# Masks built first, small loads moved, more multiplications by zero and a new order table in a window-attention and gated-convolution kernel

## The chip, the cores and the metric

The kernel runs on one NeuronCore of a Trainium2 chip. The time is that of the device, in microseconds (us), from one launch. The engines are TensorE (PE in the profile; its weight loads are a row of their own, PEld), VectorE (DVE), ScalarE (ACT), GpSimd (POOL) and SyncE (SP), which here only issues DMAs. Each engine works through its own queue in order; semaphores tie the queues together.

## The reference

Attention with four sink positions and a window of 128 for 4 batches, 8 heads, 768 positions and head size 64, and behind it a causal convolution of five taps whose sigmoid gates a projection:

```python
scores = scale * np.matmul(q, k.transpose(0, 1, 3, 2))
keep = is_sink | in_window            # pos < 4, or 0 <= row - col < 128
a = softmax(np.where(keep, scores, -1e9))
x = np.matmul(a, v)                   # heads side by side: [4, 768, 512]
gate = sigmoid(sum(conv_w[k] * x shifted by 4 - k))
val = x @ w_val
out = (gate * val) @ w_out
```

All of it in float32. n_sink and window are inputs too; the kernel computes a flag that says whether they are 4 and 128, and a general path, not taken here, stands behind it.

## The kernel before

The work is cut into 24 steps: batch (4) x blocks of 256 positions (3) x halves of the heads (2). A step has two score groups, 0 and 1. For a group, PE makes the scores of the window in 16 matmuls per pair of heads (line 298) into **one** buffer of PSUM (`ss`); DVE overwrites one triangle by a predicated copy with the mask `low` (line 303) and adds the mask and takes the row maximum in four custom operations (line 308); ACT takes four exponentials (line 316). For the step, DVE makes the reciprocal of the sums (lines 321, 322), POOL normalises (lines 330, 334), PE transposes the weights (line 346) and the sink columns (line 351), DVE applies the masks `cur` and `prev` to the transposes (lines 362, 364), ACT copies the rest (lines 355, 371), and PE multiplies by the values (lines 384, 392) into **one** buffer `xv`. ACT copies that (lines 403, 407), writes four columns of the step before at its head (line 411), POOL takes the low part of the split (line 417) and the last tap (line 421), and DVE makes four taps of the convolution from `xv` (line 429, eight operations), before ACT's tanh (line 434).

Two steps (both halves of the heads) make a pair `m`. For a pair, PE makes the projection in four parts of twelve matmuls (line 448, v0 to v3), DVE multiplies by the gate (line 459), ACT and POOL split the product in two (lines 463, 467), and PE makes the output in four parts of six (line 478, o0 to o3); ACT copies it out (line 482) and SP stores it.

The weights come as raw words of eight bytes, four chunks for each of `w_val` and `w_out`. A decode in six stages (a to f) turns each chunk into a high and a low part: ACT (line 126), three DVE operations (lines 129, 130, 132), ACT and POOL (lines 139, 140), ACT (line 135), three matmuls (lines 149 to 151), ACT (line 154). The conv weights go through a smaller decode.

The order of everything is written out by numbers. Every piece of work (a score group, a reciprocal, a load, a decode stage) is an event with a time in units of steps: `WHEN` holds the usual offset of each kind, `EARLY` the exceptions for the first and last steps, `DECODE` those of the weight chunks. The events are sorted by that number and issued in that order, so the table sets each engine's queue. Masks are an event at -9.0. In front of the events PE gets six multiplications by zero (`busy`, line 181: 128x512, bf16, results unused), and two more stand behind each score group of the first three steps. The scalars n_sink and window and the conv weights are loaded through ACT's queue before everything else.

Of the kernel before, what the change touches and what calls it, by code (L numbers as in the profile page):

```python
# [11 lines left out]
I32 = mybir.dt.int32  # L12
# [21 lines left out]
WHEN = dict(kq=-2.002, vv=1.145, s0=-0.314, e0=0.342, s1=-0.127, e1=0.504, rec=0.668, norm=0.824, tx=1.127,  # L34
            ty=1.242, sk=1.124, ev=1.474, yv=1.657, ts=1.464, val=1.842, xc=1.965, xh=2.125, hd=2.131, xl=2.311,
            c4=2.096, c0=2.268, c1=2.39, th=2.762, v0=0.37, v1=0.378, v2=0.467, g0=0.558, v3=0.567, h0=0.774,
            l0=0.947, g1=0.823, h1=1.166, l1=1.291, o0=1.375, o1=1.538, o2=1.683, t0=2.094, o3=1.887, t1=2.281,
            cw=-5.891)

EARLY = {("kq", 0): -16.694, ("vv", 0): -0.872, ("s0", 0): -8.688, ("e0", 0): -3.333, ("s1", 0): -2.548,  # L40
# [28 lines left out]
DECODE = {("wv", "l"): (-36.913, -5.959, -16.477, -1.322), ("wv", "a"): (-36.852, -1.816, -3.87, 0.468),  # L69
# [90 lines left out]
def banded(ctx, tc, wts, cw, zero, ident, flag, qt, kt, vt, vsk, w_val, conv_w, w_out, out):  # L160
# [357 lines left out]
    with tc.manual_schedule():  # L518
        for _, f, args in sorted(events, key=lambda e: e[0]):
            f(*args)  # L520
            if f is scores and args[0] < BUSY:
                busy(2)
# [200 lines left out]
```

## Time and profile before

| what | value |
|---|---|
| median of 3 runs | 293.2 us (292.97 to 293.42) |
| profiled execution, its own time | 292.72 us |
| its span, first to last instruction | 290.9 us |
| mean granted TensorE clock | 0.981 |
| PE busy | 269.0 us, 92% |
| DVE busy | 209.2 us, 72% |
| ACT busy | 179.0 us, 62% |
| POOL busy | 157.2 us, 54% |

Reading the rows: in the timeline the first number is the start in us from the beginning of the span, the second the duration; then engine, line, operation, what is written from what, shapes, and in brackets the idle time of the engine before it and what ended that. In a list of waits the three numbers are the total in us, the count and the longest. A window's row has its bounds and length, then each engine's busy time with its count of instructions, the granted clock, the DMA share and GB/s.

### The profile page before, as it was taken

How to read it: one execution, taken by the hardware profiler on the slowest of the kernel's cores; microseconds unless marked ns; L12 is line 12 of the kernel's file. 1: busy time of each engine (PE TensorE's matmuls, PEld its weight loads, DVE VectorE, ACT ScalarE, POOL GpSimd, SP SyncE). 2: the span in 40 equal slices, each digit the busy share in tenths (PEclk: the TensorE clock that was granted, in tenths of full speed). 3: DMA queues.
4: the chain of work that ended last, by engine and by line, in shares of the span. 5: the costliest groups of instructions: out<-in, count | busy, mean ns of one | idle time of the engine just before them, and what ended most of it. 6: DMA issues, size and time to landing. Idle time of an engine off the chain costs nothing. (4 is left out here: it accounts for less than half of the span.)

```text
span 290.9 us, 8754 instructions
## 1 busy us (share of the span) xinstructions
PE 269.0 (92%) x3304; PEld 222.9 (77%) x3306; DVE 209.2 (72%) x797; ACT 179.0 (62%) x613; POOL 157.2 (54%) x193
## 2 busy tenths in 40 slices
PE   3648989999999999999999999999999999999981
PEld 0324656979988879889889789899898798897860
DVE  0586899988598589687886976985885777858500
ACT  2277798686478468467655854774694676573410
POOL 2234667575555663863764564556638638645330
PEclk9966999999999999999999999999999999999999
DMA  3957926033335326418317334353362080140102
GB/s 118 362 193 244 299 94 197 7 98 91 132 96 169 114 90 200 137 38 274 98 52 227 94 128 152 97 163 116 94 183 97 2 275 2 45 139 1 74 11 72
DMA packets 27393, 36.90 MB, mean 127 GB/s; under 512 B 2256, under 2 KB 23760, under 8 KB 27344
## 3 DMA queue, kind: packets, MB, share of 16 engines
q1 hardware_dynamic: 26912, 36.25, 38.8%
q8 instruction: 28, 0.46, 0.7%
q14 instruction: 21, 0.17, 0.2%
q10 hardware_dynamic: 432, 0.02, 0.1%
HBM read 29.97 MB, written 6.29 MB: 125 GB/s over the span
## 5 line engine op out<-in xcount | busy, mean ns | idle before, releaser
L330 POOL TENSOR_TENSOR wx<-w,sm 128x512 f32<-128x512 f32 x48 | 49.2, 1047 | 73.4 <-DVE sm L322 69.8
L429 DVE SCALAR_TENSOR_TENSOR sg<-xv,cw,sg 128x256 f32<-128x256 f32 x192 | 77.4, 474 | 2.7 <-ACT xv L411 2.7
L316 ACT ACTIVATE w<-sx,ngm 128x132 f32<-128x132 f32 x192 | 74.9, 395 | 1.6 <-DVE ngm L308 1.6
L298 PE MATMUL ss<-k,q 64*64 64x200 f32 x768 | 45.8, 355 | 10.9 <-DMA q<-in_qt_dram 4.7
L403 ACT ACTIVATE xt<-xv 128x512 f32<-128x512 f32 x24 | 14.3, 597 | 64.9 <-PE xv L392 64.8
L303 DVE COPY_PREDICATED ss<-low,ss 128x256 f32<-128x256 uint8 x48 | 20.5, 426 | 43.6 <-PE ss L298 42.9
L448 PE MATMUL acc<-xh,wvh 128*128 128x256 f32 x192 | 49.1, 289 | 0.0
L448 PE MATMUL acc<-xh,wvl 128*128 128x256 f32 x192 | 47.9, 279 | 0.0
L308 DVE CUSTOM_DVE_ANT_0 sx<-ss,mask 128x132 f32<-128x132 f32 x192 | 45.2, 292 | 1.7
L298 PEld LDWEIGHTS ss<-k,q 64*64 64x64 f32 x768 | 27.0, 137 | 21.2 <-issue 10.7
L478 PE MATMUL acc<-woh,gh 128*128 128x512 f32 x96 | 40.2, 419 | 0.1
L478 PE MATMUL acc<-woh,gl 128*128 128x512 f32 x96 | 38.2, 398 | 0.6 <-POOLq L656 0.6
L478 PE MATMUL acc<-wol,gh 128*128 128x512 f32 x96 | 38.0, 396 | 0.0
L316 ACT ACTIVATION_READ_ACCUMULATOR w<-sx,ngm 128x1 f32 x192 | 36.7, 191 | 0.0
L448 PEld LDWEIGHTS acc<-xh,wvl 128*128 128x128 f32 x192 | 36.4, 190 | 0.1
L448 PEld LDWEIGHTS acc<-xh,wvh 128*128 128x128 f32 x192 | 36.0, 188 | 0.1
L467 POOL TENSOR_TENSOR gl<-sg,gh 128x512 fp32r<-128x512 f32 x24 | 30.9, 1286 | 8.1 <-ACT gh L463 6.9
L421 POOL TENSOR_TENSOR sg<-xt,cw 128x512 f32<-128x512 f32 x24 | 25.2, 1051 | 16.0 <-ACT xt L403 16.0
L392 PE MATMUL xv<-wt,v 64*64 64x192 f32 (+2 forms) x1024 | 33.3, 273 | 0.0
L392 PEld LDWEIGHTS xv<-wt,v 64*64 64x64 f32 x1024 | 31.6, 133 | 0.9
L448 PE MATMUL acc<-xl,wvh 128*128 128x256 f32 x192 | 31.1, 282 | 0.3 <-POOL xl L417 0.3
L417 POOL TENSOR_TENSOR xl<-xt,xh 128x512 fp32r<-128x512 f32 x24 | 31.0, 1293 | 0.2 <-ACT xh L407 0.2
(103 smaller groups left out, 422.3 us busy)
## 6 DMA issues: line engine op xcount, KB each, us to landing
k<-in_kt_dram SPq DMA_DIRECT2D x23, 408.0 KB, 4.0
v<-in_vt_dram SPq DMA_DIRECT2D x16, 384.0 KB, 4.5
out_dram<-osb SPq DMA_DIRECT2D x24, 256.0 KB, 2.7
q<-in_qt_dram SPq DMA_DIRECT2D x23, 256.0 KB, 4.3
raw<-in_w_val_dram SPq DMA_DIRECT2D x4, 512.0 KB, 6.4
raw<-in_w_out_dram SPq DMA_DIRECT2D x4, 512.0 KB, 5.8
v<-in_vt_dram SPq DMA_DIRECT2D x8, 256.0 KB, 4.2
vs<-in_vsk_dram SPq DMA_DIRECT2D x8, 128.0 KB, 4.1
```

The source lines that it names most:

```text
L298: nc.tensor.matmul(ss[e * D:(e + 1) * D, j, c * n:(c + 1) * n], q[js, g, (2 * c + e) * D:(2 * c + e + 1) * D], k[js, g, (2 * c + e) * HB:( ...
L303: nc.vector.copy_predicated(sv[:, :, :, :D], low[:, None, None, :].to_broadcast([P, 2, 2, D]), sv[:, :, :, 2 * HB:])
L308: nc.vector.tensor_tensor_reduce(out=sx[:, j, c], in0=sv[:, j, c, :PK], in1=mask[:, c if p == 0 else 2], op0=ALU.add, op1=ALU.min, scale=- ...
L316: nc.scalar.activation(out=w[:, g, j, c], in_=sx[:, j, c], func=AF.Exp, scale=-1.0, bias=ngm[:, g, j, c:c + 1], accum_out=sm[:, g, j, c:c ...
L330: nc.gpsimd.tensor_tensor(out=t[:, n].rearrange("p c h x -> p h c x"), in0=w[:, :, :, at], in1=sm.to_broadcast([P, 4, 2, D]), op=ALU.mult)
L392: nc.tensor.matmul(acc[o * D:(o + 1) * D, g, x0 + h * D:x0 + (h + a1 - a0 + 1) * D], v[js, g, n], t[js, g, n, a0:a1 + 1].rearrange("p a r ...
L417: nc.gpsimd.tensor_tensor(out=xl[:, g], in0=xts[s], in1=xh[:, g].bitcast(F32), op=ALU.subtract)
L421: nc.gpsimd.tensor_tensor(out=sg[s // 2][:, g], in0=xts[s], op=ALU.mult, in1=cw[:, g, KT - 1:].to_broadcast([P, 2, PQ]))
L429: nc.vector.scalar_tensor_tensor(out=g, in0=x, scalar=a, in1=g, op0=ALU.mult, op1=ALU.add)
L448: nc.tensor.matmul(acc[:, h], a[:, kc, cs], x[:, kc], start=(n == 0), stop=(n == 11))
L467: nc.gpsimd.tensor_tensor(out=gl, in0=g, in1=gh.bitcast(F32), op=ALU.subtract)
L478: nc.tensor.matmul(acc, a[:, kc, ts], x[:, kc], start=(kc + n == 0), stop=(kc + n == 5))
```

## The change

- The masks (lines 216 to 241) become the very first event (-133.1 instead of -9.0).
- The loads of n_sink and window become an event at 6.6, and the load of the conv weights an event at -31.4, behind the keys and queries of step 0; all go through SP's queue instead of ACT's. The flag comes at 21.4 instead of 24.6.
- Multiplications by zero: 16 in front instead of 6; then 6 behind the first score group, 5 behind the total of the first value chunk, 8 behind the first group of step 1 and 2 behind the total of the second value chunk, instead of 2 behind each of six score groups. That is 37 instead of 18.
- All numbers of `WHEN`, `EARLY` and `DECODE` are new. In the steady steps the order of the kinds changes in a few places; over the first four steps it changes in many.

```diff
-WHEN = dict(kq=-2.002, vv=1.145, s0=-0.314, e0=0.342, s1=-0.127, e1=0.504, rec=0.668, norm=0.824, tx=1.127,
...
+WHEN = dict(kq=-1.097, vv=-0.039, s0=-0.08, e0=0.57, s1=-0.026, e1=0.45, rec=0.712, norm=0.815, tx=1.002, ty=1.129,
...
-BUSY = 3
...
+FIRST = 16
+
+FILL = {("scores", (0, 0)): 6, ("decode_weights", ("wv", 0, 4)): 5, ("scores", (1, 0)): 8,
+        ("decode_weights", ("wv", 1, 4)): 2}
 LAG = 3
...
-def _scalars(nc, pool, n_sink, window):
-
-    raw = pool.tile([P, 2, 2], I32, name="nw_raw")
+def _scalars(nc, raw, n_sink, window):
+
     for k, ap in enumerate((n_sink, window)):
         src = ap.bitcast(I32).rearrange("(o n) -> o n", o=1)
-        nc.scalar.dma_start(out=raw[:, k, :], in_=src.to_broadcast([P, 2]))
-    return raw
+        nc.sync.dma_start(out=raw[:, k, :], in_=src.to_broadcast([P, 2]))
...
-    nc.scalar.dma_start(out=craw, in_=conv_w.bitcast(I32).rearrange("p (m t) -> p m t", t=2))
+
+    def load_conv():
+        nc.sync.dma_start(out=craw, in_=conv_w.bitcast(I32).rearrange("p (m t) -> p m t", t=2))
...
-    events += [(-9.0, masks, ()), (24.6, flag, ()), (WHEN["cw"], conv_weights, ())]
+    events += [(-133.108, masks, ()), (6.559, scalars, ()), (21.43, flag, ()), (-31.442, load_conv, ()), (WHEN["cw"], conv_weights, ())]
...
-    busy(6)
+    busy(FIRST)
     for t in skb:
         nc.gpsimd.memset(t, 0.0)
     with tc.manual_schedule():
         for _, f, args in sorted(events, key=lambda e: e[0]):
             f(*args)
-            if f is scores and args[0] < BUSY:
-                busy(2)
+            if (f.__name__, args) in FILL:
+                busy(FILL[f.__name__, args])
```

Line numbers of the changed kernel are one higher from the scores on and one lower in the masks and the decode.

What the new numbers do to the queues, first on POOL at the start of the program, before (`mk` holds the iotas of the masks, `wv_f` is the decode product of the first value chunk):

```order
L245 TENSOR_SCALAR plus<-ident 128x128
L246 TENSOR_SCALAR minus<-ident 128x128
L140 TENSOR_TENSOR wv_f<-wv_e,wv_p 128x512
L219 IOTA mk 64x64 x2
L222 IOTA mk 128x64
L140 TENSOR_TENSOR cw_f<-cw_e,cw_p 128x20
```

and in the change:

```order
L218 IOTA mk 64x64
masks.py:199 AFFINE_SELECT ident<-ident 128x128
L218 IOTA mk 64x64
L244 TENSOR_SCALAR plus<-ident 128x128
L245 TENSOR_SCALAR minus<-ident 128x128
L221 IOTA mk 128x64
L139 TENSOR_TENSOR wv_f<-wv_e,wv_p 128x512
```

The three iotas have moved ahead of the decode product. On DVE at the same place, before (the first decode's three operations, then the first of the masks):

```order
L641 MEMSET warm 128x1
L129 TENSOR_SCALAR wv_t<-wv_p 128x512
L130 SCALAR_TENSOR_TENSOR wv_t<-wv_p,wv_t 128x512
L132 TENSOR_SCALAR wv_e<-wv_t 128x512
L220 CAST mk<-mk 128x64
L221 TENSOR_SCALAR low<-mk 128x64
```

and in the change (the last of the masks, the first decode, the first score group):

```order
L237 TENSOR_SCALAR mask<-mask 128x396
L239 TENSOR_SCALAR cur<-mk 128x64
L240 TENSOR_SCALAR prev<-mk 128x64
L128 TENSOR_SCALAR wv_t<-wv_p 128x512
L129 SCALAR_TENSOR_TENSOR wv_t<-wv_p,wv_t 128x512
L131 TENSOR_SCALAR wv_e<-wv_t 128x512
L304 COPY_PREDICATED ss<-low,ss 128x2x2x64
```

All of the masks have moved ahead of the first decode, and the first score group follows that decode directly. Behind it DVE had the conv weights and a second chunk's decode ahead of the second score group; in the change the second group follows the first directly, then come the conv weights and two chunks' decodes.

The third place is DVE in a steady step with output products, before (the convolution, then the transposes' products, then the reciprocal):

```order
L308 ISA ngm 128x1
L429 SCALAR_TENSOR_TENSOR sg<-xv,cw,sg 128x256 x8
L362 TENSOR_TENSOR wt<-tr,cur 128x2x4x64
L364 TENSOR_TENSOR wt<-tr,prev 128x2x4x64
L321 TENSOR_SCALAR sm<-sm 128x8
L322 RECIPROCAL sm<-sm 128x8
```

and in the change:

```order
L309 ISA ngm 128x1
L363 TENSOR_TENSOR wt<-tr,cur 128x2x4x64
L365 TENSOR_TENSOR wt<-tr,prev 128x2x4x64
L430 SCALAR_TENSOR_TENSOR sg<-xv,cw,sg 128x256 x8
L322 TENSOR_SCALAR sm<-sm 128x8
L323 RECIPROCAL sm<-sm 128x8
```

The convolution has moved behind the transposes' products. On PE the transposes now follow the second score group of a step directly, and the sink columns' transpose stands behind the first part of the pair's products instead of ahead of the other transposes.

More of the change, by code (lines that the diff above doesn't have):

```diff
@@ L32 @@
 BIG = 1.0e30
-WHEN = dict(kq=-2.002, vv=1.145, s0=-0.314, e0=0.342, s1=-0.127, e1=0.504, rec=0.668, norm=0.824, tx=1.127,
[L35 to L40, printed above, removed]
[28 rows of a table removed]
-DECODE = {("wv", "l"): (-36.913, -5.959, -16.477, -1.322), ("wv", "a"): (-36.852, -1.816, -3.87, 0.468),
[6 rows of a table removed]
-BUSY = 3
+WHEN = dict(kq=-1.097, vv=-0.039, s0=-0.08, e0=0.57, s1=-0.026, e1=0.45, rec=0.712, norm=0.815, tx=1.002, ty=1.129,
+            sk=1.469, ev=1.109, yv=1.61, ts=1.526, val=1.923, xc=1.962, xh=2.018, hd=2.021, xl=2.251, c4=2.086,
+            c0=2.331, c1=2.619, th=2.841, v0=0.448, v1=0.549, v2=0.689, g0=0.837, v3=0.891, h0=0.913, l0=0.929,
+            g1=0.934, h1=1.069, l1=1.102, o0=1.408, o1=1.743, o2=1.893, t0=2.028, o3=2.24, t1=2.404, cw=-20.621)
+EARLY = {("kq", 0): -37.031, ("vv", 0): -2.064, ("s0", 0): -31.353, ("e0", 0): -26.169, ("s1", 0): -28.668,
[27 rows of a table added]
+DECODE = {("wv", "l"): (-66.363, -22.229, -24.294, -16.01), ("wv", "a"): (-52.963, -16.106, -22.1, -8.203),
[6 rows of a table added]
+FIRST = 16
+FILL = {("scores", (0, 0)): 6, ("decode_weights", ("wv", 0, 4)): 5, ("scores", (1, 0)): 8,
+        ("decode_weights", ("wv", 1, 4)): 2}
 LAG = 3
@@ L157, in _decode, with banded @@
     return (bias, bits, share, high) + ((add,) if unit is None else (total, low))
-def banded(ctx, tc, wts, cw, zero, ident, flag, qt, kt, vt, vsk, w_val, conv_w, w_out, out):
+def banded(ctx, tc, wts, cw, zero, ident, scalars, flag, qt, kt, vt, vsk, w_val, conv_w, w_out, out):
     nc = tc.nc
@@ L647, with scalars, flag @@
     cw = cp.tile([P, NHP, KT], F32, name="cw")
-    raw = _scalars(nc, cp, n_sink, window)
+    raw = cp.tile([P, 2, 2], I32, name="nw_raw")
     nw = cp.tile([P, 2], F32, name="nw")
     flag_i = cp.tile([P, 1], I32, name="flag_i")
+    def scalars():
+        _scalars(nc, raw, n_sink, window)
+    def flag():
+        _flag(nc, cp, raw, nw, flag_i)
     with ExitStack() as c:
-        banded(c, tc, wts, cw, zero, ident, lambda: _flag(nc, cp, raw, nw, flag_i), qt, kt, vt, vsk,
+        banded(c, tc, wts, cw, zero, ident, scalars, flag, qt, kt, vt, vsk,
                w_val, conv_w, w_out, out)
```

67 rows, old and new, of tables (DECODE, EARLY) are left out of this document.

## The prediction

> **What bounds the kernel now.** I read the windows first, cut at the places where the limits change, then the timeline at each cut.
>
> Four stretches of the span (length, busy time of each engine with instruction counts, granted TensorE clock, DMA share, GB/s):
>
> ```profile
> 0.00:8.20 8.20, 2.74 (x6) 0.72 (x6) 0.28 (x2) 2.15 (x3) 1.99 (x10) 1.00 0.48 149
> 8.20:49.10 40.90, 32.96 (x294) 18.40 (x297) 33.85 (x132) 29.52 (x94) 21.43 (x29) 0.87 0.68 223
> 49.10:271.20 222.10, 220.77 (x2934) 193.62 (x2934) 170.53 (x654) 143.21 (x511) 129.39 (x152) 1.00 0.36 114
> 271.20:290.90 19.70, 12.50 (x74) 10.15 (x72) 4.51 (x10) 4.11 (x8) 4.35 (x4) 0.97 0.16 57
> ```
>
> Order of the columns: PE, PEld, DVE, ACT, POOL. From 49.1 to 271.2 us PE works 220.8 of 222.1 us: nothing can be won there except by taking work off PE, and the change takes none off. The last 20 us are the drain. Whatever the change is worth must come from before 49.1 us, where the first value products (line 448) start:
>
> ```profile
> 48.40 0.68 DVE L364 TENSOR_TENSOR wt<-tr,prev 128x512 f32<-128x512 f32 x1
> ...
> 48.58 0.28 PE L448 MATMUL acc<-xh,wvh 128*128 128x256 f32 x1
> ```
>
> Both kernels put the same real work on PE ahead of that matmul: eight score groups, three sets of transposes, two value steps, seven decoded weight chunks. So the end moves by as much as 48.58 moves. DVE is the busiest engine on the way there, 33.85 us of 40.9, and its work is all needed. Its chain begins late:
>
> ```profile
> 9.42 0.43 DVE L132 TENSOR_SCALAR wv_e<-wv_t 128x512 int32<-128x512 int32 x1
> 10.24 1.27 POOL L140 TENSOR_TENSOR wv_f<-wv_e,wv_p 128x512 fp32r<-128x512 f32 x1 [7.58 <-ACT wv_p L139]
> 11.46 0.41 POOL L219 IOTA mk<- 64x64 int32 x2
> 11.91 0.19 DVE L220 CAST mk<-mk 128x64 f32<-128x64 int32 x1 [2.07 <-POOL mk L219]
> ...
> 14.74 0.42 DVE L303 COPY_PREDICATED ss<-low,ss 128x256 f32<-128x256 uint8 x1
> ...
> 16.06 0.08 DVE L308 DVE_READ_ACCUMULATOR2_ANT ngm<- 128x1 f32 x1
> ```
>
> The first scores were ready long before 14.74:
>
> ```profile
> 8.67 1.61 PE L298 MATMUL ss<-k,q 64*64 64x200 f32 x16 [4.75 <-DMA q<-in_qt_dram]
> ```
>
> They end at 10.28. DVE is done with the first weight chunk at 9.85, then stands 2.07 us for an iota that lies on POOL behind a decode product, then builds masks to 14.74. POOL and DVE had nothing to do before 8.2 us (1.99 and 0.28 us busy).
>
> **The change part by part.** Durations come from the execution of 292.72 us (span 290.9, 1.82 around it); it lies 0.48 under the median of 293.2, which I add back at the end.
>
> *Masks first.* The fifteen DVE operations from 11.91 to 14.74 cost 2.83 us, and the wait for POOL 2.07. In the change the iotas stand ahead of POOL's decode product and the masks ahead of DVE's first decode operation. POOL's first two iotas take 0.41 us and DVE's chain under 3, in a stretch of 8.2 us, so they are done by about 6 us. If that cover were gone they would cost the 2.83 us again. Line 303 can then start when both DVE (9.85) and PE (10.28) are there: 10.3 instead of 14.74. That is **-4.4 us** at the head of DVE's queue.
>
> *What DVE still waits for behind that.* From 14.74 to 49.08 DVE is busy 33.85 - 1.62 (first decode, 8.23 to 9.85) - 2.83 (masks) = 29.4 us and idle 4.9. With no idle time left it would finish at 10.3 + 29.4 = 39.7 (9.4 us earlier), with the same idle time at 44.6 or 44.7 (4.4 earlier). The larger pieces of the idle time, as DVE's waits give them:
>
> ```profile
> DVE wt L362 <- PE tr L346: 1.1, 1, 1.1
> DVE wv_t L129 <- PE acc L149: 0.6, 1, 0.6
> DVE wo_t L129 <- ACT wo_p L126: 0.6, 1, 0.6
> DVE ss L303 <- PE ss L298: 0.5, 1, 0.5
> ```
>
> The new order puts the second group's scores right behind the first's on DVE. There is one score buffer, so PE may write the second only when DVE has read the first (10.3 + 1.4 = 11.7, as the group above took from 14.74 to 16.14), and its sixteen matmuls take 0.91 us at full clock and 1.61 at half:
>
> ```profile
> 20.49 1.61 PE L298 MATMUL ss<-k,q 64*64 64x200 f32 x16 [2.15 <-issue]
> 29.36 0.91 PE L298 MATMUL ss<-k,q 64*64 64x200 f32 x16
> ```
>
> That adds a DVE wait of 1.0 to 1.7 us; the same happens at the second step with only a reciprocal (two operations, under 0.4 us) between, 0.6 to 1.3 us. Queued behind both are the decodes of chunks that the first value step does not need yet. Against this, the wait of 1.1 us for the transposes goes (the transposes now have a whole score group and a decode ahead of them). Adding 1.0 + 0.6 + 0.7 (second step's transposes) + 1.2 (the many small gaps) gives 3.5 us of idle time where there were 4.9, a gain of 1.4. An estimate of gaps that no row shows yet is good to about 1 us, so I count **-0.4** of it; ends: +1.5 (both pairs at half clock) and -2.5.
>
> ACT could become the limit here. From its first exponential to 48.6 its waits sum to 4.1 us:
>
> ```profile
> 16.54 0.22 ACT L139 ACTIVATE cw_p<-craw 128x20 f32<-128x20 uint32 x1 [5.75 <-DVE cw_t L130]
> ...
> 16.78 0.64 ACT L126 ACTIVATE wv_p<-raw 128x512 f32<-128x512 f32 x1
> ...
> 17.33 0.39 ACT L316 ACTIVATE w<-sx,ngm 128x132 f32<-128x132 f32 x1
> ```
>
> ```profile
> ACT w L316 <- DVE ngm L308: 1.6, 1, 1.6
> ACT xv L411 <- PE xv L392: 1.0, 1, 1.0
> ACT xv L411 <- ACT wo_p L126: 0.9, 1, 0.9
> ACT wv_p L139 <- DVE wv_t L130: 0.6, 1, 0.6
> ```
>
> So it has 31.3 - 4.1 = 27.2 us of work, plus some 1.3 for the conv weights (three operations like the one of 0.22) and one bias (0.64), which now stand behind the first exponentials. Starting at 11.0 (10.3, a copy and a first reduction) it ends at 39.5 at the earliest, level with DVE's 39.7: it allows the gain, but leaves little beyond it.
>
> *Zero multiplications.* 37 instead of 18. Sixteen stand ahead of the first keys: at half rate 16 x 0.43 = 6.9 us from 1.18 (2.74 us for six in the row below), so they end by 8.1, before the keys at 8.67. The other 21 replace 12: 9 more, 1.9 us at full rate (0.60 us for a pair, 0.17 of it the last one's tail) or 3.9 at half. They lie where PE waits for DVE's release of the scores.
>
> ```profile
> 1.18 2.74 PE L181 MATMUL acc<-zero 128*128 128x512 bf16 x6 [1.18 <-DVE warm L641]
> 30.20 0.60 PE L181 MATMUL acc<-zero 128*128 128x512 bf16 x2
> 16.25 1.13 PE L298 MATMUL ss<-k,q 64*64 64x200 f32 x16 [2.57 <-issue]
> 17.00:21.00 4.00, 1.85 (x17) 0.50 0.31 87
> 21.00:25.00 4.00, 2.74 (x25) 0.50 0.92 308
> ```
>
> From 17 to 25 us PE ran at half clock, after a hole of 2.57 us that ended at 16.25. If the new ones keep the clock full, each score group is there 0.7 us sooner, but DVE is mostly the later one. Taken as 0, with an end of -1.0. The six behind the first scores take 1.3 us at full rate, inside the 1.4 of DVE; at half rate 2.6, and the second scores come 1.1 us late and take 0.7 longer.
>
> *Loads.* The two scalars and the conv weights go from ACT's queue to SP's; ACT loses three issues like the one below, where it has nothing else. The conv weights (128 x 40 words, 0.02 MB) now come behind the first keys and are needed at about 13 us. The value chunks and the first two steps' keys keep their order. 0.
>
> ```profile
> 1.14 0.45 ACTq L91 DMA_DIRECT2D nw_raw<-in_window_dram  x1
> ```
>
> *Steady order.* On DVE the transposes' products (lines 362, 364) now stand ahead of the conv (line 429). PE must not start the next value step (line 384) before the conv has read the old one. In a half with output products:
>
> ```profile
> 140.43 0.91 PE L298 MATMUL ss<-k,q 64*64 64x200 f32 x16
> 147.34 0.62 PE L384 MATMUL xv<-skt,vs 64*64 64x128 f32 x16
> 142.73 3.22 DVE L429 SCALAR_TENSOR_TENSOR sg<-xv,cw,sg 128x256 f32<-128x256 f32 x8
> 145.87 0.68 DVE L362 TENSOR_TENSOR wt<-tr,cur 128x512 f32<-128x512 f32 x1
> 147.06 0.16 DVE L321 TENSOR_SCALAR sm<-sm 128x8 f32<-128x8 f32 x1
> ```
>
> Swapped, the conv ends 1.19 us later (145.87 to 147.06), at about 147.1, and line 384 follows at 147.34: 0.2 us to spare. I take 0; ends: +2 (a tenth of a microsecond in each of some twenty steps, for the sink transpose that now breaks into a run of other matmuls) and -1.3, the idle time of PE in the stretch.
>
> *Tail.* The flag's nine small operations leave the last steps; the wait they caused goes, **-0.3**:
>
> ```profile
> 267.99 0.43 PEld L384 LDWEIGHTS xv<-skt,vs 64*64 64x64 f32 x16 [0.36 <-DVE nw L100]
> ```
>
> Sum: -4.4 - 0.4 - 0.3 = -5.1. 292.72 - 5.1 = 287.6 in that execution, **288.1 us** as a median.
>
> **The rivals.**
>
> *Half clock stays (0.15).* PE is idle from the end of the sixteen to 8.67. If they warm up halfway they end near 6.4, and the hole is 2.3 us; the hole that ended the full clock here was 2.57 us. For it: the two are alike. Against: afterwards PE has more to do than before. Price: 1.1 + 0.7 at the first pair, about 0.7 at the next, 2.5 us: 290.6. The Trainium skill, "TensorE: Matmul & The Clock Gate", section "What's actually happening", says that the clock falls only after a whole idle window of about 3.4 us, and that the window runs freely; by that rule the hole of 2.3 us leaves the clock full and the price is 0. The trace agrees only loosely, since a hole of 2.57 us was enough here.
>
> *More than the head (0.10).* DVE's remaining waits shrink too, by 2 us: 286.1. For it: 4.9 us of idle time are there. Against: ACT's bound of 39.5 and the two new waits.
>
> *The start is bound elsewhere (0.08).* The head start is eaten by ACT and by POOL's decode products, which stand ahead of the first normalisation on POOL in the new order. Against: POOL has 19.5 idle microseconds of 40.9. Time 292.7, within what can be told from no change (0.2%, about 0.6 us).
>
> *The conv holds PE (0.12), slower.* The 0.2 us to spare are not there, in each of eleven halves with output products. It decides against the change from 5.1 / 11 = 0.46 us per half; with 0.6 us the total is +6.6 - 5.1 = +1.5: 294.7. For it: DVE waits for the score matmuls, PE for the conv, so a shortfall returns in every round. Against: in the row pair above it fits.
>
> **How the numbers follow.** The forecast has 0.55. Faster by over 0.2%: 0.55 + 0.15 + 0.10 = 0.80, with 0.01 of the fourth; within 0.2%: 0.07; slower: 0.12. The range for 8 in 10 goes from 285.8 (286.1 less a little of the spread on the second term) to 292.4, which leaves out the slower case and part of the third; the forecast's own range is 286.5 to 289.8.
>
> **What would show it.** Masks on DVE before 8 us and the first line 303 at 10.2 to 10.8; first value products at 43 to 45 us instead of 48.58; PE busy above 99% from there to the tail, as many microseconds long as before; clock 1.00 rather than 0.50 in 17 to 25 us. Wrong would be: line 303 early but the first value products still at 47 or later (third rival), or a new PE wait on DVE ahead of line 384 (fourth).

## The result, and the profile after

The changed kernel takes **285.75 us** (median of 4 runs, 285.2 to 286.4), the kernel before beside it 293.13 (292.97 to 293.42): a ratio of 0.9748, 95% interval 0.9725 to 0.9771. The forecast was 288.1. The direction was right; the gain is 7.4 us instead of 5.1, and the time lies 0.05 below the lower end of the range (285.8 to 292.4). All medians and spreads here leave out four executions that ran far slower than the rest of the same kernel (304 to 662 us).

The profiled execution took 286.40 us, with a span of 284.3. The four stretches of the span, cut at the same places of the work as before (0.5 us behind the first value product, 19.7 ahead of the end; columns: length, busy time of PE, PEld, DVE, ACT and POOL with instruction counts, granted clock, DMA share, GB/s):

```profile
0.00:8.20 8.20, 7.02 (x32) 2.71 (x32) 4.40 (x20) 3.37 (x5) 3.06 (x14) 1.00 0.68 215
8.20:41.40 33.20, 28.86 (x295) 16.91 (x290) 30.02 (x114) 28.44 (x89) 22.42 (x26) 1.00 0.85 286
41.40:264.60 223.20, 220.53 (x2933) 193.08 (x2933) 170.96 (x654) 145.77 (x513) 129.33 (x152) 1.00 0.33 110
264.60:284.30 19.70, 12.90 (x75) 10.17 (x73) 4.60 (x10) 4.26 (x9) 4.55 (x4) 0.97 0.16 57
```

The second stretch is 33.2 us long instead of 40.9, and DVE is busy for 30.0 of it: masks and first decode now lie in the first stretch, and what is left has little idle time. Its clock is 1.00, where it stood at 0.87 before. The steady stretch is 1.1 us longer: PE is idle 2.67 us of it, before 1.33.

The timeline of the changed kernel at the start:

```profile
1.18 6.40 PE L180 MATMUL acc<-zero 128*128 128x512 bf16 x16 [1.18 <-DVE warm L642]
4.86 0.67 ACT L125 ACTIVATE wv_p<-raw 128x512 f32<-128x512 f32 x1 [2.63 <-DMA raw<-in_w_val_dram]
7.51 0.91 PE L299 MATMUL ss<-k,q 64*64 64x200 f32 x16
8.49 0.43 DVE L304 COPY_PREDICATED ss<-low,ss 128x256 f32<-128x256 uint8 x1 [1.31 <-PE ss L299]
10.97 0.43 DVE L304 COPY_PREDICATED ss<-low,ss 128x256 f32<-128x256 uint8 x1 [1.07 <-PE ss L299]
...
40.88 0.28 PE L449 MATMUL acc<-xh,wvh 128*128 128x256 f32 x1
```

The kernel before reads its first weight chunk here:

```profile
7.54 0.66 ACT L126 ACTIVATE wv_p<-raw 128x512 f32<-128x512 f32 x1 [4.42 <-DMA raw<-in_w_val_dram]
```

Against the rows of before: ACT reads the first weight chunk at 4.86 instead of 7.54, the first scores start at 7.51 instead of 8.67 and take 0.91 instead of 1.61, the first copy under the mask comes at **8.49** instead of 14.74 (forecast: 10.3), and the first value product at **40.88** instead of 48.58. In the two profiled executions (286.40 and 292.72) the difference of 6.32 splits so: -6.25 up to the first copy, -1.45 from there to the first value product (33.84, now 32.39), **+1.10** from there to the end of the span (242.32, now 243.42), +0.28 around the span. These executions lie at opposite sides of their medians, hence 6.3 here and 7.4 there.

The last positive term has rows of its own. In the changed kernel's timeline, at the output products of one pair:

```profile
236.38 0.68 DVE L460 SCALAR_TENSOR_TENSOR sg<-sg,acc 128x512 f32<-128x512 f32 x1
237.10 0.63 ACT L464 ACTIVATE gh<-sg 128x512 fp32r<-128x512 f32 x1 [1.52 <-DVE sg L460]
237.78 0.50 PE L479 MATMUL acc<-woh,gh 128*128 128x512 f32 x1 [0.25 <-ACT gh L464]
239.14 0.50 PE L479 MATMUL acc<-woh,gl 128*128 128x512 f32 x1 [0.62 <-POOL gl L468]
```

DVE multiplies the gate so late that PE stands 0.25 us for ACT's half of it and 0.62 for POOL's. The kernel before has no such row there (no wait of PE between 231 us and the end of this stretch).

### The profile page after: what moved, and what is told of

The parts are those of the page before. It is cut to its first block, busy times and chain, and to the rows that moved or that the text cites. A ratio compares the mean times of both kernels' runs of the same rounds, so it can differ in the third digit from the quotient of the medians.

```text
span 284.3 us, 8772 instructions
## 1 busy us (share of the span) xinstructions
PE 269.3 (95%) x3323; PEld 222.9 (78%) x3325; DVE 210.0 (74%) x797; ACT 181.8 (64%) x613; POOL 159.4 (56%) x193
## 5 line engine op out<-in xcount | busy, mean ns | idle before, releaser
L299 PE MATMUL ss<-k,q 64*64 64x200 f32 x768 | 43.6, 341 | 3.1 <-DVE ngm L309 2.7
L299 PEld LDWEIGHTS ss<-k,q 64*64 64x64 f32 x768 | 26.2, 132 | 12.5 <-issue 6.8
```

Source lines behind the costliest of these rows:

```text
L299: nc.tensor.matmul(ss[e * D:(e + 1) * D, j, c * n:(c + 1) * n], q[js, g, (2 * c + e) * D:(2 * c + e + 1) * D], k[js, g, (2 * c + e) * HB:( ...
```

## The experiments

Theory at the start: masks first is worth what the prediction says, and what came on top is from the small loads (theory L) and the zero multiplications (theory C). The rival gives all of it to the masks. Every kernel below was timed beside the kernel before; those of one group ran on one chip, and each heading has the kernel before's median in that group. Line numbers move by a few from kernel to kernel.

This table gathers what the paragraphs below read from it (us; the last three columns from the profile of each).

| kernel | time (lowest to highest) | first copy under mask | first value product | from there to the span's end |
|---|---|---|---|---|
| before | 293.13 (292.97 to 293.42) | 14.74 | 48.58 | 242.3 |
| changed, e1 | 285.65 (285.38 to 286.13) | 7.93 | 40.33 | 243.7 |
| e2 loads back | 287.52 (287.33 to 287.78) | 9.47 | 41.86 | 243.6 |
| e3 zeros back | 287.53 (287.39 to 287.93) | 7.44 | 41.41 | 243.9 |
| e4 masks back | 291.76 (291.65 to 292.23) | 12.13 | 45.73 | 243.9 |
| f1 masks alone | 288.00 (287.25 to 288.58) | 9.92 | 43.25 | 242.5 |
| f2 loads alone | 291.17 (290.82 to 291.56) | 11.94 | 47.59 | 242.2 |
| f3 zeros alone | 292.42 (291.1 to 292.75) | 14.53 | 47.50 | 242.3 |
| f4 all but the tables | 283.76 (283.47 to 284.38) | 7.13 | 39.28 | 242.5 |
| g1 changed again | 286.28 (285.38 to 286.65) | 8.32 | 40.72 | 243.5 |
| g2 = f4 again | 283.92 (283.26 to 284.34) | 8.54 | 40.44 | 242.2 |
| h1 ten zeros | 285.22 (284.91 to 285.39) | 7.45 | 39.82 | 243.5 |
| h2 ten zeros, old tables | 283.47 (283.34 to 284.21) | 7.41 | 39.33 | 242.3 |

### One part taken back at a time (the kernel before: 292.79)

**e1**, the changed kernel itself:

> The changed kernel again, as the anchor for the three beside it. All theories: 285 to 286.5 us, first value product at 40.9 us of the span, ratio to before 0.973 to 0.977.

285.65, ratio 0.9744 (0.9713 to 0.9775). This is what the next three are compared with.

**e2**, the small loads back on ACT's queue at the front:

```diff
-    def load_conv():
-        nc.sync.dma_start(out=craw, ...)
+    nc.scalar.dma_start(out=craw, ...)
...
-        nc.sync.dma_start(out=raw[:, k, :], in_=src.to_broadcast([P, 2]))
+        nc.scalar.dma_start(out=raw[:, k, :], in_=src.to_broadcast([P, 2]))
...
-    events += [(-133.108, masks, ()), (6.559, scalars, ()), (21.43, flag, ()), (-31.442, load_conv, ()), ...]
+    events += [(-133.108, masks, ()), (21.43, flag, ()), ...]
+    scalars()
```

> The changed kernel with its three small loads (n_sink, window, conv weights) issued through ACT's queue ahead of everything, as before. Theory L (the small loads hold up the first weight chunk and the first keys): the first chunk is read at 7.5 us instead of 4.9, the first keys at 8.7 instead of 7.5, the first copy on DVE starts near 9.9 instead of 8.5, and the kernel is 1.2 to 2.7 us slower than the changed one: 287 to 288.5. Rival (the loads cost nothing, as the prediction had it; the earlier chunk is a matter of chance): within 0.4 us of the changed kernel.

287.52, so 1.87 us more: theory L. Three loads of 22 KB in all delay the first copy by 1.54. How, the transfers show. Windows of the kernel before, which has these loads at the same place (bounds, length, granted clock, DMA share, GB/s):

```profile
3.00:4.00 1.00, 1.00 0.28 90
4.00:5.00 1.00, 1.00 0.40 116
5.00:6.00 1.00, 1.00 0.58 168
```

and of the changed kernel (e1):

```profile
3.00:4.00 1.00, 1.00 0.97 319
4.00:5.00 1.00, 1.00 1.08 385
5.00:6.00 1.00, 1.00 1.02 352
```

Up to 3.05 us the same large loads are issued at the same times in both. With the small ones beside them the transfer engines are less than half busy until 5 us and move between a quarter and a half of the bytes. In e2 itself the three shares are 0.53, 0.35 and 0.77 (166, 80 and 227 GB/s): better at first than in the kernel before, and still far below e1.

**e3**, the zero multiplications as before (6 at the start, 2 behind each of the first six score groups):

```diff
-FIRST = 16
-FILL = {("scores", (0, 0)): 6, ("decode_weights", ("wv", 0, 4)): 5, ("scores", (1, 0)): 8, ("decode_weights", ("wv", 1, 4)): 2}
+FIRST = 6
+FILL = {("scores", (s, g)): 2 for s in range(3) for g in range(2)}
```

> The changed kernel with the multiplications by zero as before: six in front, two behind each score group of the first three steps, none elsewhere. Theory C (they keep the clock full, and half clock would cost the start): granted clock 0.5 somewhere between 8 and 25 us, score groups of 1.61 us instead of 0.91 there, first value product 1.5 to 3 us later, 287 to 289. Rival (DVE is the later one anyhow, the clock costs nothing): within 0.5 us of the changed kernel. Rival of the other sign (they stand in the way): faster by 0.3 to 1 us.

287.53, 1.88 us more: theory C's size. Its timeline:

```profile
5.77 1.61 PE L298 MATMUL ss<-k,q 64*64 64x200 f32 x16 [1.85 <-DMA q<-in_qt_dram]
8.96 1.61 PE L298 MATMUL ss<-k,q 64*64 64x200 f32 x16 [0.60 <-PE acc L179]
10.62 0.43 DVE L303 COPY_PREDICATED ss<-low,ss 128x256 f32<-128x256 uint8 x1 [1.77 <-PE ss L298]
...
13.28 0.46 DVE L127 TENSOR_SCALAR wv_t<-wv_p 128x512 int32<-128x512 int32 x1 [0.73 <-PE acc L147]
...
18.10 0.91 PE L298 MATMUL ss<-k,q 64*64 64x200 f32 x16 [3.00 <-DVE ngm L308]
```

Two score groups run at the slow rate, and DVE waits 1.77 for the second instead of 1.07. Then it waits 0.73 for a product of the first decode (line 147), which it does not in e1. From the first copy to the first value product it takes 33.97 instead of 32.40, 1.57 more. The granted clock of 0.5 that was expected with it is not in the profile: it is shown as 1.00 from 8 to 30 us, and only the durations of the matmuls tell the rate. But the keys are used at 5.77, while in e1 PE is in its sixteen zeros until 7.03: the sixteen also hold something up (taken up with h1).

**e4**, the masks back to their place in the sequence, ahead of the first score group and with the iotas behind the decode product on POOL:

```diff
-    events += [(-133.108, masks, ()), ...
+    events += [(-31.4, masks, ()), ...
-          ... ("wv", "c"): (-29.386, ...
+          ... ("wv", "c"): (-31.41, ...
```

> The changed kernel with the masks right ahead of the first score group and the decode product of the first chunk ahead of the iotas on POOL, as before; loads, fills and the rest stay new. Theory M (the masks at the head of DVE's queue were the largest piece): the decode product ends near 8.9 us, iotas and masks run from there to 12.0, the first copy on DVE starts at 12.0 instead of 8.5, and 3 to 3.6 us are lost: 288.7 to 289.4. Rival (the slack of DVE behind the head takes up half of it): 287 to 288.

291.76, 6.1 us more; the 3 to 3.6 expected was too little. Its timeline:

```profile
9.31 0.20 DVE L219 CAST mk<-mk 128x64 f32<-128x64 int32 x1 [2.08 <-POOL mk L218]
...
12.13 0.42 DVE L304 COPY_PREDICATED ss<-low,ss 128x256 f32<-128x256 uint8 x1
...
13.64 1.61 PE L299 MATMUL ss<-k,q 64*64 64x200 f32 x16 [4.33 <-issue]
```

The first copy is 4.20 later than in e1. That is the wait for the iota (2.08) and the masks (2.82) of the kernel before, less the 0.75 that DVE waits for the first scores in e1: 4.15. The rest is TensorE: it stands 4.33 us, and then runs at half clock, as the windows of e4 have it:

```profile
14.00:16.00 2.00, 2.00 (x17) 1.05 (x10) 0.66 (x4) 1.25 (x6) 0.00 (x0) 0.50 1.04 381
16.00:18.00 2.00, 2.00 (x5) 0.77 (x4) 1.84 (x13) 0.33 (x2) 0.58 (x2) 0.50 0.11 45
```

which makes the way to the first value product 1.2 us longer. So the masks' 4.2 and the clock's 1.2 hang together: without masks first, the zeros are too few to fill the hole. These two make 5.4 of the 5.57 by which the two profiled executions differ; the medians differ by 6.1.

### One part put in at a time (the kernel before: 292.67)

**f1**, the masks alone: `(-9.0, masks, ())` becomes `(-100.0, masks, ())` in the kernel before.

> The kernel before (about 293.0 us here) with the masks alone moved to the front; the small loads stay ahead on ACT's queue, the zero multiplications and the table stay as before. The first copy under the mask (14.74 us in the kernel before) should come once the first scores are there, at 10.2 to 10.8, as the prediction's first term has it. Theory S (each part brings its own share, masks -4.2, the difference between the first copies with masks back and with all parts in the runs so far, 12.13 and 7.93): 288.5 to 289.2. Theory X (without the loads moved the masks gain nothing, since the first chunk and the first keys are then the bound): above 291. Theory C (the masks also take away the half clock that stood at 17.6 to 27 us, since the hole of 2.57 us in TensorE's work ahead of the second score group goes): 287 to 288, with a granted clock of 1.00 in 18 to 26 us.

288.00, ratio 0.9829 (0.9775 to 0.9882): the upper end of theory C. This is the prediction's first term by itself:

```profile
8.25 1.61 PE L298 MATMUL ss<-k,q 64*64 64x200 f32 x16 [4.33 <-DMA q<-in_qt_dram]
9.92 0.43 DVE L303 COPY_PREDICATED ss<-low,ss 128x256 f32<-128x256 uint8 x1 [0.47 <-PE ss L298]
```

The copy comes when the first scores are there, 4.8 earlier, and the time falls by 4.7 (the interval allows 3.5 to 6.6): 4.4 had been forecast for it. Theory C's sign is there as well: the granted clock is 1.00 from 16 us on, a score group takes 0.91 at 16.26, where the kernel before still has 1.61 at 20.49, and the way from the first copy to the first value product is 0.5 shorter (33.33).

**f2**, the small loads alone (the edit of e2 the other way round, in the kernel before):

> The kernel before with only the small loads moved off ACT's queue onto SP's, behind the first keys and queries. First chunk read by ACT at 4.8 to 4.9 instead of 7.54, first keys at 5.8 instead of 8.67. Theory L (the three small loads hold up the first chunk, and everything behind it on VectorE, masks included, comes 2.7 earlier): first copy at 12.0 to 12.2, 290.0 to 290.7. Theory L' (the loads only brought 1.5, what undoing them in the changed kernel cost to the first copy): 291.2 to 291.8. Theory N (worth nothing without the masks): 292.6 to 293.2.

291.17, ratio 0.9937 (0.9915 to 0.9958): -1.5, at the edge of theory L'.

```profile
4.74 0.66 ACT L124 ACTIVATE wv_p<-raw 128x512 f32<-128x512 f32 x1 [2.51 <-DMA raw<-in_w_val_dram]
9.11 0.20 DVE L218 CAST mk<-mk 128x64 f32<-128x64 int32 x1 [2.07 <-POOL mk L217]
...
11.94 0.42 DVE L302 COPY_PREDICATED ss<-low,ss 128x256 f32<-128x256 uint8 x1
...
13.45 1.56 PE L297 MATMUL ss<-k,q 64*64 64x200 f32 x16 [2.84 <-issue]
```

The first chunk and the first copy do come 2.8 earlier, as theory L has it, but the first value product only 1.0: TensorE is at half clock for longer. After the hole of 2.84 us the granted clock is 0.50 from 14 to 26 us, in the profile of the kernel before from 18 to 26.

**f3**, the zero multiplications alone (the edit of e3 the other way round):

> The kernel before with only the zero multiplications of the change (16 first, then 6, 5, 8, 2). The first copy under the mask stays at 14.7, since VectorE's masks end it. Theory H (a hole of some 2.5 us or more stays ahead of the second score group, and the half clock behind it stays too): 292.6 to 293.4, granted clock 0.50 in 18 to 26 us. Theory K (the zeros alone close the hole and keep full clock): 291.0 to 291.8 and clock 1.00 there.

292.42, ratio 0.9979 (0.9957 to 1.0002): not to be told from no change. Theory H: with the masks late, holes stay that the zeros don't fill, and the granted clock is 0.50 from 18 to 24 us.

```profile
15.99 0.91 PE L301 MATMUL ss<-k,q 64*64 64x200 f32 x16 [2.80 <-DVE ngm L311]
20.28 1.61 PE L301 MATMUL ss<-k,q 64*64 64x200 f32 x16 [3.38 <-issue]
```

**f4**, all three, and the tables of times (WHEN, EARLY, DECODE) and the flag's place of the kernel before:

> The kernel before with masks first, small loads on SP's queue behind the keys and the zero multiplications of the change, but the tables of times of the kernel before. The rest up to the changed kernel is the tables' own share. Theory T0 (the new tables bring nothing of their own): within 0.6 of 285.7. Theory T+ (the new early order brings 1 us or more: it puts the second and third score groups ahead): 286.7 to 289. Theory T- (the new tables cost about 1.3 in the steady part, as the time from the first value product to the end says, 243.4 to 243.9 against 242.3): 284.2 to 285.1.

**283.76**, ratio 0.9686 (0.964 to 0.9733), under everything that the three theories allowed (T-, the nearest, had 284.2 to 285.1), and 1.9 under the changed kernel: the new tables cost time. One by one the three parts bring 4.7, 1.5 and 0.25, in sum 6.4; together 8.9. The 2.5 between is what the parts give each other, above all the zeros once the masks are first (1.9 in e3, nothing clear of noise in f3).

### What the new tables cost (the kernel before: 292.78)

**g1** and **g2** are the changed kernel and f4 once more, side by side.

> The changed kernel once more, beside the three that follow. 285.4 to 286.1, first value product at 40.3 to 40.9, from there to the end of the span 243.4 to 243.9.

> Once more the kernel with masks, small loads and zero multiplications of the change, and the tables of times of the kernel before, now beside the changed kernel on one chip. If the new tables cost time: 283.5 to 284.4, that is 1.3 to 2.3 under the changed kernel; if the earlier difference was one of chips: within 0.5 of it.

286.28 (0.2 above what was expected) against 283.92, 2.4 us apart (1.9 across the two earlier groups): no difference of chips. The table above shows where: from the first value product to the end 243.5 to 243.9 with the new tables, 242.2 to 242.5 with the old, and some **1.2 us in the steady part** between kernels that differ in the times of the events alone (e1 and f4, g1 and g2, h1 and h2: 1.15 to 1.3). From the first copy to the first value product it is 32.4 (e1, g1) against 32.15 and 31.9 (f4, g2), some 0.3 to 0.5. Another 0.3 lies around the span: time and span of the profiled executions differ by 2.08 to 2.17 with the new tables and by 1.74 to 1.82 with the old; it goes with the later times (1.77 in g3, 2.08 in g4 below), and no run shows what it is. Each of g1 and g2 has slow zeros at its start, which f4 has not:

```profile
1.18 5.04 PE L182 MATMUL acc<-zero 128*128 128x512 bf16 x16 [1.18 <-DVE warm L643]
...
7.13 0.43 DVE L305 COPY_PREDICATED ss<-low,ss 128x256 f32<-128x256 uint8 x1
```

is f4's timeline, and g2's, of the same kernel:

```profile
1.18 6.45 PE L182 MATMUL acc<-zero 128*128 128x512 bf16 x16 [1.18 <-DVE warm L643]
...
8.54 0.43 DVE L305 COPY_PREDICATED ss<-low,ss 128x256 f32<-128x256 uint8 x1 [1.36 <-PE ss L300]
```

**g3** and **g4** cross the tables: new times for the start and old ones behind, and the other way round.

```diff
-WHEN, EARLY of one kernel
+EARLY of the one kernel for steps 0 to 7 and pairs 0 to 2 (g4: 0 to 5 and 0 to 1), WHEN and EARLY of the other behind them
```

> The changed kernel with the new times for the first eight steps (and the first three pairs), the decode of the weights and the loads, and the times of the kernel before for all steps behind them. Theory A (the new tables lose 1.2 in the steady part, in the products into line 479 that wait 0.9 for POOL's and ACT's halves of the gate, and the rest in the start): 284.2 to 284.9, no such wait left in 230 to 245 us. Theory B (all of the loss is in the start, where the first copy under the mask comes 0.8 later): 285.4 to 286.1.

> Tables of the kernel before for the first six steps and two pairs and for the decode, the new times behind them, with masks, small loads and zero multiplications of the change. Theory A: 284.7 to 285.4, with the wait of 0.9 at line 479 back. Theory B: 283.4 to 284.3.

Neither time can be used: 290.36 and 291.82, slower than both parents. The join of two tables has a price of its own, as g3's timeline shows:

```profile
99.77 0.91 PE L269 MATMUL ss<-k,q 64*64 64x200 f32 x16 [1.96 <-DVE ngm L279]
105.87 0.30 PE L322 MATMUL acc<-ident,skb 128*128 128x128 f32 x1 [2.02 <-ACT osb L453]
```

(In g3 the tanh of step 7 also falls behind the product that uses it, so one half of a pair is gated with the value before its tanh; nothing is left out.) Far behind the join the rows can still be compared. Windows of g3, with the old steady times (length, PE busy, clock, DMA share, GB/s):

```profile
200.00:250.00 50.00, 49.59 (x667) 1.00 0.30 96
```

and of g4, with the new ones:

```profile
200.00:250.00 50.00, 48.71 (x653) 1.00 0.27 87
```

0.88 us of idle time go with the new steady times, whatever stands at the start, and g4's timeline has the waits of 0.25 and 0.62 at the output products again (at 241.65 and 243.01), g3's has not. With a wait of 0.38 at 260 us (line 479 again, for ACT's copy of the sink transpose), which stands in the profiles of the changed kernel and in none with the old tables, that makes 1.25, about the whole of the 1.2. (Four of the profiles with the old tables, f1, f4, g2 and h2, have a wait of 0.3 for POOL near there instead, so the account closes to 0.3 us.)

### The zeros ahead of the first keys, and the small loads one by one (the kernel before: 292.67)

**h1** (`FIRST = 10` in the changed kernel) and **h2** (the same in f4):

> The changed kernel with 10 zero multiplications at its start instead of 16. In the profiles so far the 16 took 5.0 to 6.4 us from 1.18, while the first keys and queries had landed by 5.8. Theory F (the 16 hold the first scores up by what they last beyond 5.8): the ten end by 5.5, first scores at 5.8 to 6.0, first copy under the mask at 7.1 to 7.6, time 284.7 to 285.5. Theory W (with ten the rate of the first scores is the slow one, 1.61 a group, and what follows is slow too, as with six): first copy at 7.4 but 286.5 to 287.6.

> The kernel with the old tables of times, masks first, small loads on SP's queue and the zero multiplications of the change, with 10 instead of 16 at the start. Theory F: 0.3 to 0.9 under the 283.9 that it takes with 16, so 283.0 to 283.6. Theory W: 284.5 or more.

285.22, 0.4 to 1.1 under the three medians of the changed kernel; 283.47, 0.3 to 0.5 under those of f4, whose runs overlap with it. Theory F, at its weak end, and as a time not shown beyond doubt: the changed kernel itself ran in other groups, and three of the thirteen executions of the changed kernel lie within h1's four. The timeline of h1:

```profile
1.18 4.45 PE L180 MATMUL acc<-zero 128*128 128x512 bf16 x10 [1.18 <-DVE warm L642]
5.84 1.54 PE L299 MATMUL ss<-k,q 64*64 64x200 f32 x16 [0.22 <-DMA q<-in_qt_dram]
7.45 0.43 DVE L304 COPY_PREDICATED ss<-low,ss 128x256 f32<-128x256 uint8 x1 [0.28 <-PE ss L299]
```

The scores start with the keys at 5.84, slowly, and end at 7.38 where e1's ended at 7.87 and the first profile's at 8.42. Six zeros fewer let the scores start 1.1 to 1.7 earlier, of which 0.6 is given back, since the scores then run at the slow rate (1.54 instead of 0.91). But sixteen can be as good: with them the first copy comes at 7.13 (f4), 7.35 (i1) and 7.49 (h4) where the rate rises early, and at 8.49 and 8.54 (first profile, g2) where it rises late. Ten, with 7.45 and 7.41 (h2), take away the late cases and do not beat the early ones.

**h3** has only the two scalars on ACT's queue at the front, **h4** only the conv weights:

> The changed kernel with only the two scalar loads (n_sink and window, broadcast to 128 rows, 1 KB each) back on ACT's queue at the front. All three small loads there cost 1.87 us, and the first read of a weight chunk went from 4.81 to 7.25. Theory S (the broadcast scalars, which land 4.0 and 5.7 after their issue, do the damage): first read of a chunk at 6.5 or later and 287.0 to 287.7. Theory B (each small load does its part): first read 5.6 to 6.5, 286.2 to 286.9. Theory V (it is the conv weights): 285.4 to 286.1.

> The changed kernel with only the load of the conv weights (20 KB, 160 bytes a row) back on ACT's queue at the front. Theory S: 285.4 to 286.1, first read of a weight chunk at 4.8 to 5.0. Theory B: 286.0 to 286.7. Theory V: 287.0 to 287.7, first read at 6.5 or later.

h3 takes 287.49 and h4 286.14, which is within the changed kernel's three medians: theory S. In h4 the chunk is read at 4.80, in h3 at

```profile
7.06 0.66 ACT L125 ACTIVATE wv_p<-raw 128x512 f32<-128x512 f32 x1 [3.94 <-DMA raw<-in_w_val_dram]
```

with h3's windows as poor as those of the kernel before:

```profile
3.00:4.00 1.00, 1.00 0.46 138
4.00:5.00 1.00, 1.00 0.37 89
5.00:6.00 1.00, 1.00 0.82 267
```

The two loads carry 2 KB, in 288 packets by the profile's list of queues.

**i1** and **i2** (the kernel before: 292.66) ask what it is about them. i1 puts as many pieces of the same size, 8 bytes, on ACT's queue, but each from its own address:

```diff
+    cview = conv_w.bitcast(I32).rearrange("p (m t) -> p m t", t=2)
+    for j in (0, 1):
+        nc.scalar.dma_start(out=craw[:, j:j + 1, :], in_=cview[:, j:j + 1, :])
     def load_conv():
-        nc.sync.dma_start(out=craw, in_=...)
+        nc.sync.dma_start(out=craw[:, 2:, :], in_=cview[:, 2:, :])
```

i2 leaves the three small loads on SP's queue and issues them ahead of the first chunk (`scalars` and `load_conv` at -90 and -80).

> The changed kernel with two small loads on ACT's queue at the front in the place of the two scalars: the first and the second 8 bytes of every row of the conv weights, 128 rows 160 bytes apart, so as many and as small pieces as the scalars have, but each from an address of its own (the rest of the conv weights follows on SP's queue). Theory A (the scalars did harm because their 128 pieces all read one address): first read of a weight chunk at 4.8 to 5.0, 285.4 to 286.3. Theory P (it is the number of tiny pieces): first read at 6.5 or later, 287.2 to 287.9, as with the scalars.

> The changed kernel with the three small loads on SP's queue, but ahead of the first weight chunk, keys and queries. Theory Q (it takes a second queue beside the large loads for the harm): each load takes its issue alone, the first read of a weight chunk comes some 1.2 later, at 5.8 to 6.2, 286.2 to 287.2. Theory T (the two broadcast loads hold up what shares the transfer engines with them, whichever the queue): first read at 6.8 or later, 287.3 to 289.

i1: 286.17, theory A. Its timeline and its windows:

```profile
4.97 0.69 ACT L125 ACTIVATE wv_p<-raw 128x512 f32<-128x512 f32 x1 [1.85 <-DMA raw<-in_w_val_dram]
```

```profile
3.00:4.00 1.00, 1.00 0.78 239
4.00:5.00 1.00, 1.00 1.07 383
```

Again 288 packets on ACT's queue, and the large loads hardly notice. So it is not the number or the size of the pieces; what is left between h3 and i1 is their source, in h3 the same 8 bytes for all 128 rows, and the tile that they are written to, which no run tells apart from it. i2: 286.90, theory Q, with the read 0.2 later than expected:

```profile
2.12 0.66 SPq L260 DMA_DIRECT2D raw<-in_w_val_dram  x1
...
6.41 0.66 ACT L125 ACTIVATE wv_p<-raw 128x512 f32<-128x512 f32 x1 [4.18 <-DMA raw<-in_w_val_dram]
```

The chunk is issued 1.39 later than in e1 and read 1.60 later. Ahead of the large loads, on their own queue, the broadcasts cost little more than their three issues; beside them, on another queue, they cost 2.2 (4.81 to 7.06 in the read, h3). Why the loads of a repeated address are slow, and why they harm less in i2, no run shows.

## Why the prediction was right, and where it was wrong

**Masks first, -4.4.** Right. f1 measures -4.7 with the copy at 9.92, where 10.3 was forecast; the 0.4 are the keys of that execution (8.25, before 8.67). In the changed kernel the masks lie in 2.0 to 5.6 us, where DVE has nothing else to do.

**Loads, 0.** This step failed: a term put at nothing, which the runs put at 1.5. It counted ACT's three issues and when the conv weights are needed, and did not ask what these transfers do to the others. It took the arrival of the first keys (8.67) and the first chunk (7.54) as given; f2 measures -1.5 for the move alone, e2 +1.87 for taking it back. The rows to see it were there before: ACT waited 4.42 us for a chunk issued at 0.74, with the transfer engines 0.28 to 0.58 busy. The Trainium skill, "DMA: Bandwidth & Descriptors", section "Issuing engines are not separate DMA queues", says that transfers of all issuing engines run on the same 16 engines and interleave. The runs agree in so far as two small loads on ACT's queue slow the large ones on SP's: from 3 to 4 us the engines are 0.97 busy in e1 and 0.46 in h3.

**Zero multiplications, taken as 0, with an end of -1.0.** This step failed in size. Alone they bring nothing clear of noise (f3), behind masks that come first 1.9 (e3). The step supposed that "DVE is mostly the later one". In e3 it is not: DVE waits 0.70 longer for the second scores and 0.73 for a product of the decode, which the slow rate lengthens too, and in all 1.6 is lost between the first copy and the first value product. "They end by 8.1, before the keys at 8.67" held for the zeros (7.58) and failed for the keys, which now come at 5.8: the sixteen hold the scores up, and the first copy with them, in the first profile by about a microsecond (8.49, with ten 7.45 in h1), in the profiles where the rate rises early by nothing.

**What DVE still waits for, -0.4 (ends +1.5 and -2.5).** The sum came within the ends, at -1.45, near the 1.4 that the rows had given before they were cut to 0.4. But it isn't the new order of DVE's work that brings it, so this is luck: with the old tables the stretch is 0.3 to 0.5 shorter still (f4, g2). It is the zeros: with theirs as before (e3) the stretch is 33.97, 0.1 from the 33.84 of the kernel before.

**Steady order, 0 (ends +2 and -1.3).** Failed in size, within its ends: **+1.2**. The place named for a loss, the conv ahead of the next value step, costs nothing: the weight loads of line 385 wait for it once, 0.37 at 261.56 us, as they did once for 0.3 in the kernel before, and no matmul waits there. The loss is elsewhere, mostly in one pair whose gate is multiplied too late (0.87 at line 479, and 0.38 in another), which the one pair of halves that the prediction looked at could not show.

**Tail, -0.3.** Nothing of it came. The row it rests on is one of weight loads (PEld), which waited while the matmul before them still ran: from 267 to 269 us PE is busy without a gap. In the changed kernel the flag's wait is gone and the one of 0.37 for the conv stands in its place.

**The rivals.** "Half clock stays" did not come: the sixteen last until 7.58 and the first scores start at 7.51, so there is no hole, and the clock is 1.00. Where such a hole did stand ahead of the first scores, 2.32 us in f3, they took 0.91 all the same. Half clock after a longer hole is in e4, which lacks the early masks: 4.33 us, and it costs 1.2 there, where 2.5 was forecast for the rival. The rule of the Trainium skill beside it ("TensorE: Matmul & The Clock Gate", section "What's actually happening", an idle window of about 3.4 us) fits the runs as loosely as before: holes of 2.80 us in f3 and 3.00 in e3 left the next score group at 0.91, one of 3.38 in f3 was followed by 1.61, and 2.57 in the kernel before and 2.84 in f2 were enough for half clock. "More than the head" gave the time nearest to the result, 286.1, but not by its mechanism alone: of its two microseconds in DVE's waits 1.45 came, and the rest of the surplus is the keys and the chunk. The start was not bound elsewhere, and the conv does not hold PE. Of the signs that were named, the masks were done before 8 us and the clock was 1.00; the first copy and the first value product came earlier than the ranges given for them (8.49 and 40.88), and PE was busy 98.8% of the steady stretch instead of above 99%.

By the runs the sum reads: masks -4.7, loads -1.5, zeros -0.25, what the three give each other -2.5, together -8.9; the tables +1.9 (e1 against f4; +2.4 for g1 against g2), which leaves -7.0, and e1 measures -7.1. Of this the prediction had the first term, and neither the other gains nor the loss. The gains that it missed are about twice the loss that it missed; that the forecast lies only 2.3 us from the result is luck. With the old tables and ten zeros, 283.47 beats both kernels (ratio 0.9692, 0.9671 to 0.9713).

## What to carry to other kernels

When work is waiting on a first load, read the bandwidth of the transfers while it waits: engines that are half idle with large loads issued are a reason to look for something small in their way, which here was a broadcast from one address. An early part and an ordering table that came with it are worth measuring apart: here the parts brought 8.9 us and the table took 1.9 to 2.4 back. The same filler on TensorE brought 1.9 us where it raised the rate before the first scores and nothing dropped it again (e1 against e3), and nothing clear of noise where a hole of 3.38 us stayed (f3), and in the profiles where it outlasted the load that the first scores wait for, it held them up.

## What the runs showed of the hardware

- Two loads of 1 KB, each 8 bytes broadcast to 128 rows, on ACT's queue beside the large loads held the transfers to 89 to 138 GB/s between 3 and 5 us where 319 to 385 are reached without them (h3, e1). The same number of 8-byte pieces from addresses of their own left 239 to 383 (i1).
- Sixteen zero multiplications of the same shape, all started at 1.18, lasted 4.96 (f3) to 6.45 us (g2) in all, with a granted clock shown as 1.00 all along; the same kernel had 5.04 once and 6.45 once (f4, g2). So a filler sized to end with a load's arrival can miss it by more than a microsecond. The Trainium skill, "TensorE: Matmul & The Clock Gate", section "What's actually happening", says that the moment at which the clock rises differs from run to run, and the traces agree.
- Early in these profiles the duration of a known group of matmuls tells the rate and the granted clock does not: in e3 score groups take 1.61 at 5.77 and 8.96 and 0.91 at 18.10, under a clock shown as 1.00 throughout.
